# Wider weight rows, shared load slots and a one-row last piece in a decode kernel that streams weights

## Chip, cores, metric

One core of one Trainium2 chip runs the kernel. The metric is device microseconds of one execution. A kernel is executed several times; runs called "fast" are those of the undisturbed state, and all comparisons below use them alone. Kernels timed together share one chip and one set of runs of the kernel before.

## The reference, cut to what matters

```python
# two tokens (batch 2), D = 576, 32 query heads, 16 KV heads, head size 128, last 2048 of 8192 positions
xn  = layernorm(x)
q   = xn @ wq                                  # wq: 576 x 4096
p   = softmax(q . k_cache[:, :, -2048:] * Dh**-0.5)
att = (p . v_cache[:, :, -2048:]) @ wo         # wo: 4096 x 576
h   = relu(xn @ w1 + b1) ** 2                  # w1: 576 x 4608
out = x + att + h @ w2 + b2                    # w2: 4608 x 576
```

Everything is bf16. K, V and the four weight matrices are 53.6 MB and each byte is used once, for two tokens: a kernel that is all loading.

## The kernel before

It works on eight units (four groups of four KV heads, two batches). For each unit it loads K and V (128 partitions, 16 KB rows), transposes K on TensorE, multiplies scores, softmax, and P times V. wq, w1, wo and w2 are loaded between them; w2 comes last. The parts that the change touches:

```python
kvpool = tile_pool(bufs=6)       # K, V and w2 pieces, 16 KB per partition
wbig   = tile_pool(bufs=4)       # full 128-row blocks of wq, later of w1, 9 KB per partition
...
def issue_w(tiles, wt, c, name, width, lrem):
    if c < NFULL:                # NFULL = 4: rows c*128 .. c*128+127, one row to a partition
        tl = wbig.tile([P, WBW], BF16, tag="wbig", name=f"{name}_{c}")
        nc.sync.dma_start(out=tl[:, 0:width], in_=wt[c * P:(c + 1) * P, :])
    ...                          # the last 64 rows of 576 go to a tile of their own
...
W2P = [(0, 0, 9), (0, 9, 18), (1, 0, 9), (1, 9, 15), (1, 15, 18)]   # w2 pieces: half, first and last row of 18
...
for i, w in enumerate(W2P):      # after the last P times V: per row of a piece two 128x2x288 matmuls
    mlp_o(*w, last=(i == len(W2P) - 1))
fin_sb = copy(out_ps); two output DMAs of 1.1 KB
```

All big loads are issued by SyncE on one queue, in program order.

## Time and profile before

| what | before |
|---|---|
| time, median | 137.42 us (137.30 to 137.44, 3 runs) |
| span of the profiled run | 135.6 us |
| DMA engines busy with data (q1) | 94.7% of the span |
| TensorE busy | 76% |
| bytes, mean rate | 53.90 MB, 397 GB/s |
| last data packet (trace) | 131.82 us |
| final copy of the output begins | 132.87 us |

A page shows the span in 40 slices; a digit is the busy share of a slice in tenths.

### The profile page before, as it was taken

What the parts mean: (1) busy time and instruction counts of PE and PEld (TensorE: products, weight loads), DVE (VectorE), ACT (ScalarE), POOL (GpSimd) and SP (SyncE); (2) the same over time, 40 slices, a digit from 0 to 9 for tenths busy, and PEclk for the clock granted to TensorE, in tenths of its full rate; (3) what the DMA queues carried; (4) which work ended last, traced back from release to release, by engine and by line L of the source; (5) the groups of instructions that cost most, each with busy time, mean ns of one, the idle gap of its engine ahead of it and who ended that gap; (6) DMA issues with size and microseconds to landing.
All of it is one profiled execution on the core that took longest, in us unless ns stands there. A gap on an engine that the chain in (4) does not pass through costs nothing.

```text
span 135.6 us, 4461 instructions
## 1 busy us (share of the span) xinstructions
PE 102.5 (76%) x2054; PEld 91.9 (68%) x2054; DVE 53.9 (40%) x124; ACT 43.0 (32%) x47; POOL 10.0 (7%) x31
## 2 busy tenths in 40 slices
PE   1049947599968999879943993999399599768961
PEld 0039947589968999839933993688399479664530
DVE  7502421574352325422653446355634645660001
ACT  6705550165012521004701550272155127110000
POOL 6400000110110001100011001101100110110000
PEclk9999985569855685556985698698559959955599
DMA  5999999999999999999999999999999999999940
GB/s 112 418 419 418 428 442 402 420 429 440 430 393 430 438 411 409 444 425 396 440 440 406 445 420 425 404 443 423 425 430 413 430 415 426 422 410 417 393 166 1
DMA packets 5278, 53.90 MB, mean 397 GB/s; under 512 B 630, under 2 KB 652, under 8 KB 1164
## 3 DMA queue, kind: packets, MB, share of 16 engines
q1 hardware_dynamic: 5188, 53.61, 94.7%
q8 instruction: 16, 0.26, 0.8%
q0 software_dynamic: 64, 0.01, 0.0%
q14 instruction: 2, 0.02, 0.0%
q10 hardware_dynamic: 8, 0.00, 0.0%
HBM read 53.62 MB, written 0.00 MB: 395 GB/s over the span
## 4 chain that ended last, share of the span: by engine, by line
DMA 55%; PE 35%; DVE 3%; issue 2%; POOL 1%; ACT 1%; SPq 1%; POOLq 0%; ACTq 0%
DMA k<-in_A_k_cache_dram 41%; PE kT_ps L237 18%; DMA w<-in_B_w_dram 10%; PE hT_ps L323 5%; DMA b_sb<-in_B_b_dram 4%; PE sc_ps L252 4%; PE out_ps L213 4%; PE oT_ps L289 3%; PE qT_ps L225 1%; ACT kT L240 1%; POOL b_sb L146 1%; DVE l L271 1%; DVE sub L266 1%; SPq L94 0%; DVE fin_sb L414 0%
## 5 line engine op out<-in xcount | busy, mean ns | idle before, releaser
L237 PE MATMUL kT_ps<-ident,k 128*128 128x128 bf16 x512 | 47.3, 260 | 9.9 <-DMA k<-in_A_k_cache_dram 9.9
L237 PEld LDWEIGHTS <-k 128*128 128x128 bf16 x512 | 39.6, 119 | 11.8 <-DMA k<-in_A_k_cache_dram 10.7
L240 ACT COPY kT<-kT_ps 128x1024 bf16<-128x1024 bf16 x32 | 32.3, 1012 | 40.1 <-PE kT_ps L237 40.0
L242 DVE COPY kT<-kT_ps 128x1024 bf16<-128x1024 bf16 x32 | 22.0, 690 | 33.4 <-PE kT_ps L237 33.4
L252 PE MATMUL sc_ps<-qT_all,kT 128*128 128x8 bf16 x512 | 21.6, 168 | 1.6 <-ACT kT L240 0.8
L252 PEld LDWEIGHTS <-kT 128*128 128x128 bf16 x512 | 19.1, 100 | 2.6 <-ACT kT L240 1.2
L289 PE MATMUL oT_ps<-pT,v 128*128 128x8 bf16 x512 | 15.5, 167 | 1.9 <-issue 1.4
L269 ACT ACTIVATE pT<-sub 128x512 bf16<-128x512 f32 x8 | 5.0, 630 | 35.1 <-DVE sub L266 35.1
L289 PEld LDWEIGHTS <-v 128*128 128x128 bf16 x512 | 14.4, 99 | 2.1 <-issue 1.6
L271 DVE TENSOR_REDUCE l<-pT 128x8 f32<-128x512 bf16 x8 | 8.5, 1066 | 4.2 <-ACT pT L269 4.2
L213 PE MATMUL out_ps<-wo,ws 128*2 128x288 bf16 x64 | 8.3, 438 | 2.4 <-DVE ws L309 2.4
L323 PE MATMUL hT_ps<-xnT,w 128*128 128x2 bf16 x144 | 9.8, 201 | 0.0
L323 PEld LDWEIGHTS <-w 128*128 128x128 bf16 x144 | 9.4, 165 | 0.0
L258 DVE TENSOR_REDUCE m<-sc_ps 128x8 f32<-128x512 f32 x8 | 5.5, 692 | 9.7 <-PE sc_ps L252 9.7
L262 POOL PARTITION_ALL_REDUCE gmax<-m x8 | 2.9, 364 | 84.8 <-DVE m L260 84.8
L213 PE MATMUL out_ps<-w,hT_sb 128*2 128x288 bf16 x72 | 6.9, 353 | 1.3 <-DMA w<-in_B_w_dram 1.3
L213 PEld LDWEIGHTS <-ws 128*2 128x2 bf16 x64 | 3.5, 115 | 5.4 <-DVE ws L309 2.8
L213 PEld LDWEIGHTS <-hT_sb 128*2 128x2 bf16 x72 | 3.8, 103 | 4.3 <-issue 1.9
L266 DVE TENSOR_TENSOR sub<-sc_ps,gm 128x512 f32<-128x512 f32 x8 | 5.5, 692 | 0.3
L225 PE MATMUL qT_ps<-xnT,wq 128*128 128x2 bf16 x128 | 4.0, 165 | 2.2 <-DMA wq<-in_A_wq_dram 1.9
L225 PEld LDWEIGHTS <-wq 128*128 128x128 bf16 x128 | 3.9, 103 | 2.2 <-DMA wq<-in_A_wq_dram 2.0
L273 POOL PARTITION_ALL_REDUCE lsum<-l x8 | 3.2, 398 | 24.5 <-DVE l L271 24.5
(58 smaller groups left out, 35.1 us busy)
## 6 DMA issues: line engine op xcount, KB each, us to landing
v<-in_A_v_cache_dram SPq DMA_DIRECT2D x8, 2048.0 KB, 28.4
k<-in_A_k_cache_dram SPq DMA_DIRECT2D x7, 2048.0 KB, 29.4
w<-in_B_w_dram SPq DMA_DIRECT2D x4, 1152.0 KB, 17.7
wo<-in_A_wo_dram SPq DMA_DIRECT2D x4, 1152.0 KB, 27.4
wq<-in_A_wq_dram SPq DMA_DIRECT2D x4, 1024.0 KB, 6.9
w<-in_B_w_dram SPq DMA_DIRECT2D x3, 1296.0 KB, 22.7
k<-in_A_k_cache_dram SPq DMA_DIRECT2D x2, 1024.0 KB, 9.1
w<-in_B_w_dram SPq DMA_DIRECT2D x1, 864.0 KB, 15.7
```

The lines of the kernel that those rows point to most:

```text
L213: nc.tensor.matmul(out_ps[32 * i:32 * i + B, :], lhsT=lhsT, rhs=rhs_of(i * OH, (i + 1) * OH), start=start, stop=stop, skip_group_check=True)
L225: nc.tensor.matmul(qT_ps[:, h, :], lhsT=lhsT, rhs=xnT[:, xc, :], start=(c == 0 and h == 0), stop=(c == KC - 1), skip_group_check=True)
L237: nc.tensor.transpose(out=kT_ps[:, i * P:(i + 1) * P], in_=k_sb[:, j * Dh:(j + 1) * Dh], identity=ident[:])
L240: nc.scalar.copy(out=kT[:], in_=kT_ps[:])
L242: nc.vector.tensor_copy(out=kT[:], in_=kT_ps[:])
L252: nc.tensor.matmul(sc_ps[:, g * JG + i, :], lhsT=kT[:, i * P:(i + 1) * P], rhs=qT_all[:, b, tq * NC:(tq + 1) * NC], start=True, stop=True)
L258: nc.vector.tensor_reduce(out=m1[:], in_=sc_ps[:].rearrange("p j c -> p c j"), axis=AX.X, op=ALU.max)
L266: nc.vector.tensor_tensor(out=sub[:], in0=sc_ps[:], in1=gm2[:].unsqueeze(1).to_broadcast([P, NJ, NC]), op=ALU.subtract)
L269: nc.scalar.activation(out=pT[:], in_=sub[:], func=ACT.Exp, scale=scale)
L271: nc.vector.tensor_reduce(out=l1[:], in_=pT[:].rearrange("p j c -> p c j"), axis=AX.X, op=ALU.add)
L289: nc.tensor.matmul(oT_ps[:], lhsT=v_sb[:, j * Dh:(j + 1) * Dh], rhs=pT_tiles[u][:, j, :], start=(j == 0), stop=(j == NJ - 1))
L323: nc.tensor.matmul(hT_ps[:, s * FR + r, :], lhsT=lhsT, rhs=xnT[:, xc, :], start=(c == 0 and s == 0 and r == 0), stop=(c == KC - 1), skip_g ...
```

## The change

The intent is fewer and larger packets (a packet is the run of bytes, here one row, that a DMA engine moves at a time). The 512 full rows of wq and w1 are laid out as row 4p+i, so that partition p holds rows 4p to 4p+3 and a load can fetch two neighbouring rows as one run of 16 or 18 KB. The activations are transposed with a stride of 4 to match. All big loads share seven 18 KB slots, and the last w2 piece shrinks to one row.

```diff
-    kvpool = ctx.enter_context(tc.tile_pool(name="kvpool", bufs=6))
+    kvpool = ctx.enter_context(tc.tile_pool(name="kvpool", bufs=7))
-    wbig = ctx.enter_context(tc.tile_pool(name="wbig", bufs=NFULL))
+    RP = NFULL // 2
+    SLOT = max(UE, RP * F)
 ...
+    def issue_w(tiles, wt, c0, c1, name, width):
+        if c0 % RP == 0:
+            tiles[c0 // RP] = kvpool.tile([P, SLOT], BF16, tag="kv", name=f"{name}_{c0 // RP}")
+        tl = tiles[c0 // RP]
+        rows = wt[0:NFULL * P, :].rearrange("(p i) l -> p (i l)", i=NFULL)
+        o = (c0 % RP) * width
+        nc.sync.dma_start(out=tl[:, o:o + (c1 - c0) * width], in_=rows[:, c0 * width:c1 * width])
 ...
-        nc.tensor.transpose(out=pro_ps[:, c, :], in_=xn_sb[:, c * P:(c + 1) * P], identity=ident[:B, :B])
+        nc.tensor.transpose(out=pro_ps[:, c, :], in_=xn_sb[:, c:NFULL * P:NFULL], identity=ident[:B, :B])
 ...  (loads: wq row 0, both halves of K 0, wq row 1, wq rows 2-3; w1 rows 0-1, w1 rows 2-3)
-    W2P = [(0, 0, 9), (0, 9, 18), (1, 0, 9), (1, 9, 15), (1, 15, 18)]
+    W2P = [(0, 0, 9), (0, 9, 18), (1, 0, 9), (1, 9, 17), (1, 17, 18)]
 ...  (start: q block 0, all transposes of K 0, then the other q blocks)
```

More of the change, by code (lines that the diff above doesn't have):

```diff
@@ L81 @@
     k_tiles, v_tiles, wq_tiles, w1_tiles, wo_tiles, w2_tiles = {}, {}, {}, {}, {}, {}
-    WBW = max(Hq * Dh, F)
     WRW = max(LQ, L1)
+    RP = NFULL // 2
+    SLOT = max(UE, RP * F)
     def unit_view(cache, u):
@@ L89, in issue_kv @@
     def issue_kv(tiles, cache, u, name, parts=1):
-        tl = kvpool.tile([P, UE], BF16, tag="kv", name=f"{name}_{u}")
+        tl = kvpool.tile([P, SLOT], BF16, tag="kv", name=f"{name}_{u}")
         v = unit_view(cache, u)
@@ L95, in issue_kv, with issue_rem, w_operands @@
                 for i in range(parts)]
-    def issue_w(tiles, wt, c, name, width, lrem):
-        if c < NFULL:
-            tl = wbig.tile([P, WBW], BF16, tag="wbig", name=f"{name}_{c}")
-            nc.sync.dma_start(out=tl[:, 0:width], in_=wt[c * P:(c + 1) * P, :])
-        else:
-            tl = wrem.tile([P, WRW], BF16, tag="wrem", name=f"{name}_rem")
-            nc.sync.dma_start(out=tl[:, 0:lrem], in_=wt[NFULL * P:D, :].rearrange("r (s l) -> (r s) l", s=S))
-        tiles[c] = tl
-    def issue_wq(c):
-        issue_w(wq_tiles, A_wq, c, "wq", Hq * Dh, LQ)
-    def issue_w1(c):
-        issue_w(w1_tiles, B_w1, c, "w1", F, L1)
-    def w_operands(tiles, c, col0, L, step=1):
+    def issue_w(tiles, wt, c0, c1, name, width):
[5 more added lines that the diff above has]
+        nc.sync.dma_start(out=tl[:, o:o + (c1 - c0) * width], in_=rows[:, c0 * width:c1 * width])
+    def issue_rem(tiles, wt, name, lrem):
+        tl = wrem.tile([P, WRW], BF16, tag="wrem", name=f"{name}_rem")
+        nc.sync.dma_start(out=tl[:, 0:lrem], in_=wt[NFULL * P:D, :].rearrange("r (s l) -> (r s) l", s=S))
+        tiles["rem"] = tl
+    def w_operands(tiles, c, col0, width, L, step=1):
         last = col0 + (P - 1) * step
         if c < NFULL:
-            return tiles[c][:, col0:last + 1:step], c
+            o = (c % RP) * width
+            return tiles[c // RP][:, o + col0:o + last + 1:step], c
         sg = col0 // L
         assert last // L == sg
-        return tiles[c][:, col0 - sg * L:last - sg * L + 1:step], NFULL + sg
+        return tiles["rem"][:, col0 - sg * L:last - sg * L + 1:step], NFULL + sg
     def issue_wo(tq):
@@ L126, in issue_w2 @@
     def issue_w2(s, r0, r1):
-        tl = kvpool.tile([P, (r1 - r0) * D], BF16, tag="kv", name=f"w2_{s}_{r0}")
+        tl = kvpool.tile([P, SLOT], BF16, tag="kv", name=f"w2_{s}_{r0}")
         rows = B_w2[s * L1:(s + 1) * L1, :].rearrange("(p r) n -> p (r n)", r=FR)
-        nc.sync.dma_start(out=tl[:], in_=rows[:, r0 * D:r1 * D])
+        nc.sync.dma_start(out=tl[:, 0:(r1 - r0) * D], in_=rows[:, r0 * D:r1 * D])
         w2_tiles[(s, r0)] = tl
@@ L138 @@
     k0 = issue_kv(k_tiles, A_k_cache, 0, "k", parts=2)
-    issue_wq(0)
+    issue_w(wq_tiles, A_wq, 0, 1, "wq", Hq * Dh)
     k0[0]()
-    issue_wq(1)
     k0[1]()
-    for c in range(2, KC):
-        issue_wq(c)
+    issue_w(wq_tiles, A_wq, 1, 2, "wq", Hq * Dh)
+    issue_w(wq_tiles, A_wq, 2, 4, "wq", Hq * Dh)
+    issue_rem(wq_tiles, A_wq, "wq", LQ)
     b1_sb = const.tile([P, S, FR], BF16, name="b1_sb")
@@ L223, in q_block @@
         for h in range(Hq):
-            lhsT, xc = w_operands(wq_tiles, c, h * Dh, LQ)
+            lhsT, xc = w_operands(wq_tiles, c, h * Dh, Hq * Dh, LQ)
             nc.tensor.matmul(qT_ps[:, h, :], lhsT=lhsT, rhs=xnT[:, xc, :],
@@ L321, in mlp_h_block @@
             for r in range(FR):
-                lhsT, xc = w_operands(w1_tiles, c, s * L1 + r, L1, FR)
+                lhsT, xc = w_operands(w1_tiles, c, s * L1 + r, F, L1, FR)
                 nc.tensor.matmul(hT_ps[:, s * FR + r, :], lhsT=lhsT, rhs=xnT[:, xc, :],
@@ L347, in load_v @@
             f()
-    W2P = [(0, 0, 9), (0, 9, 18), (1, 0, 9), (1, 9, 15), (1, 15, 18)]
+    W2P = [(0, 0, 9), (0, 9, 18), (1, 0, 9), (1, 9, 17), (1, 17, 18)]
     load_k(1)
-    issue_w1(0)
-    issue_w1(1)
+    issue_w(w1_tiles, B_w1, 0, 2, "w1", F)
     load_v(0)
     load_k(2)
-    for c in range(2, KC):
-        issue_w1(c)
+    issue_w(w1_tiles, B_w1, 2, 4, "w1", F)
+    issue_rem(w1_tiles, B_w1, "w1", L1)
     load_v(1)
@@ L360 @@
     load_k(3)
-    nxt = {0: [], 1: [], 2: [lambda: load_v(2), lambda: load_k(4)]}
     def step(u, extra=()):
@@ L372, in step @@
         softmax(u)
-    for g in range(4):
+    q_block(0)
+    for g in range(NG):
         transposes(0, g)
-    q_block(0)
-    q_block(1)
-    for g in range(4, NG):
-        transposes(0, g)
-    for c in range(2, KC):
+    for c in range(1, KC):
         q_block(c)
@@ L404 @@
                 load_k(u + 2)
-        if u >= NU - 1:
-            pass
         if u == NU - 1:
```

## The prediction

The medians of 309 to 613 ns are times of packets in the trace of before. For the instruction fetches what stands is the count, 16 packets on q8 for the 4110 TensorE instructions (the page lists 4108); for the clock it is what was granted, 0.50 from 120 to 128 us and 1.00 from 129 us to the last matmul.

> **What bounds the kernel now.** I read the page's slices first, because they say whether one resource is full all the time.
>
> ```profile
> span 135.6 us, 4461 instructions
> PE   1049947599968999879943993999399599768961
> PEclk9999985569855685556985698698559959955599
> DMA  5999999999999999999999999999999999999940
> DMA packets 5278, 53.90 MB, mean 397 GB/s; under 512 B 630, under 2 KB 652, under 8 KB 1164
> q1 hardware_dynamic: 5188, 53.61, 94.7%
> q8 instruction: 16, 0.26, 0.8%
> ```
>
> The DMA row is 9 in every slice from the second to the 38th; the PE row falls to 3 several times. So the sixteen DMA engines set the pace and TensorE waits. 94.7% of 135.6 us is 128.4 us of packets per engine, and the data packets run from about 1.7 us to 131.8 us. There is no hole in the stream that a better order of loads could fill. The second view is the DMA queue's own waits, since the change moves buffers:
>
> ```profile
> SPq L94 <- PE kT_ps L237: 17.0, 3, 6.5
> SPq L129 <- PE kT_ps L237: 14.8, 2, 8.4
> SPq L100 <- PE qT_ps L225: 10.9, 4, 4.5
> ```
>
> These waits look large (10.9 us for w1 loads behind the reads of wq, which the change removes in this form), but a wait of the issuing queue costs time only if the engines run dry, and the slices say that they do not. The page's issue list gives the reserve:
>
> ```profile
> v<-in_A_v_cache_dram SPq DMA_DIRECT2D x8, 2048.0 KB, 28.4
> k<-in_A_k_cache_dram SPq DMA_DIRECT2D x7, 2048.0 KB, 29.4
> w<-in_B_w_dram SPq DMA_DIRECT2D x1, 432.0 KB, 13.0
> ```
>
> A K or V load lands 28 to 29 us after its issue, while 2 MiB (2.097 MB) at some 425 GB/s take 5 us: more than 20 us of other loads stand ahead of it. The third view is the end, as busy time by stretch (PE, PEld, DVE, ACT, POOL with counts, then granted clock, DMA share, GB/s) and as the TensorE timeline:
>
> ```profile
> 110.00:120.00 10.00, 8.38 (x203) 7.89 (x202) 5.19 (x11) 4.68 (x5) 0.38 (x2) 0.84 1.01 425
> 128.00:129.00 1.00, 0.88 (x12) 0.43 (x7) 0.00 (x0) 0.00 (x0) 0.00 (x0) 0.81 0.83 332
> 129.00:130.00 1.00, 0.84 (x14) 0.61 (x15) 0.00 (x0) 0.00 (x0) 0.00 (x0) 1.00 0.58 227
> 130.00:131.00 1.00, 0.43 (x8) 0.17 (x3) 0.00 (x0) 0.00 (x0) 0.00 (x0) 1.00 0.48 183
> 131.00:132.00 1.00, 0.77 (x12) 0.52 (x12) 0.00 (x0) 0.00 (x0) 0.00 (x0) 1.00 0.32 124
> ```
>
> ```profile
> 125.66 3.22 PE L213 MATMUL out_ps<-w,hT_sb 128*2 128x288 bf16 x28
> 129.16 1.27 PE L213 MATMUL out_ps<-w,hT_sb 128*2 128x288 bf16 x18 [0.28 <-DMA w<-in_B_w_dram]
> 131.24 0.90 PE L213 MATMUL out_ps<-w,hT_sb 128*2 128x288 bf16 x12 [0.81 <-DMA w<-in_B_w_dram]
> 132.30 0.53 PE L213 MATMUL out_ps<-w,hT_sb 128*2 128x288 bf16 x6 [0.17 <-DMA w<-in_B_w_dram]
> ```
>
> From 128.5 us the DMA share is about a half: eight engines have finished and eight run 3.1 us longer. Sorting the packet records of the trace into sixteen sequences, each with every load's eight packets in order, I find that the engines ending at 131.7 to 131.8 us each carried two of the 16 instruction fetches (queue q8) and the others none. A fetch leaves a gap of about 1.05 us in the data, and the data packet after it takes up to 0.55 us too long: about 1.55 us each, 3.1 us for two. The kernel's end is the slowest engine's last packet, 0.5 us to landing, six matmuls, and the output.
>
> [...]medians are 309 ns for 8192 B, 349 for 9216, 398 for 10368, 613 for 16384. The line through 9216 and 16384 has 0.0368 ns per byte and some 10 ns left over. [...]PE has 4110 instructions in both kernels, [...]and the trace shows 16 packets of 16384 B on q8. [...]The granted clock of 1.00 at the end and 0.50 from 120 to 128 us [...]matters in the tail below.
>
> **The change, part by part.**
>
> *Wider rows.* w1 used 4 x 128 packets of 9216 B and will use 2 x 128 of 18432 B. From the line an 18432 B packet takes 613 + 2048 x 0.0368 = 688 ns (an estimate; no such packet is in this trace) in place of 2 x 349 = 698. Each engine carries 16 of them: 16 x 10 = 0.16 us. Two wq loads become one with 16384 B rows: 8 packets at 613 in place of 16 at 309, 8 x 5 = 0.04 us. The other two wq loads keep 8192 B. Three loads fewer mean three completion packets of 9 ns fewer per engine: 0.03 us. Bytes are unchanged. Together 0.23 us off every engine, the eight late ones too.
>
> *Row order 4p+i.* The activations are transposed with a stride of 4 to match; counts of matmuls and transposes stay the same, and so do the column strides of the weight loads. Each partition now reads its row from an address 32 or 36 KB after the last one's. K reads at 16 KB steps run at 613 ns, so I take no loss.
>
> *Seven shared slots.* SBUF goes from 6 x 16 + 4 x 9 = 132 KB to 7 x 18 = 126 KB per partition. The second w1 load now waits for the slot of K 0, which is free when its 64 transposes are done, by some 17 us; V 1 and K 3 wait for wq's slots at 18 to 22 us. At that time 15.4 MB have been issued (wq 4.7, K 0 to 2 and V 0 8.4, half of w1 2.4), which last until 1.7 + 15.4/0.425 = 38 us. Later a load waits for the buffer seven loads back in place of six. So the engines stay fed and the value is 0.
>
> *Load and PE order at the start.* TensorE does one q block, all eight transpose groups, then the other q blocks. K 0 arrives whole before the second wq row. TensorE waits for K 1 at 25.9 us in any case, so 0.
>
> *The last w2 piece.* 9+9+9+6+3 rows become 9+9+9+8+1. The packet time is 264 + 139 before and about 349 + 52 after (1152 B, estimated from 31 ns at 576 B and 139 at 3456 B): nothing. But the eight-row piece lands later than the six-row one did. The last landing, 132.26 before, comes at 132.03. The one-row piece takes 8 x 52 + 9 = 0.43 us of its engine, so the eight-row piece lands at 131.60. Its 16 matmuls take 16 x 75 ns (0.90 us for 12 above) = 1.20, and the last two 0.18: end at 132.98, where before it was 132.83. With the last piece so small, its landing no longer sets the end; the eight-row piece does. The cost is 0.38 against the 0.23 won.
>
> Sum: -0.23 + 0.38 = +0.15 us with the full clock. If the half-rate clock (3.22 us for 28 matmuls, 115 ns) covers the tail, 18 x 115 = 2.07 in place of 1.38: another +0.7 us.
>
> **Rivals.** (a) Wide rows run better than the line says, or the freed 10.9 us of queue wait count. Against it: [...]no dry slice. [...](b) The 32 KB step of wq collides in HBM. If wq and w1 (9.4 MB, 22 us) ran 10% slower, the end would move by 2.2 us, to 139.6. Nothing in the trace speaks for it: V, K and wo with different steps all lie on one line. (c) The shared slots starve the queue around 20 to 45 us. A hole would come out one to one in the end, 138 to 140. The 15 MB issued early speak against it. (d) A fetch no longer hits the late engines twice, or the last fetch comes after the data: up to 1.5 us off, to 136. But it needs all eight late engines to change, and the PE instruction count has not. (e) The clock in the tail, above: 138.2.
>
> **Range and chances.** The centre weighs +0.15 us (full clock), +0.85 (half clock, less likely since low activity at the end stood at 1.00 before) and a slightly better packet rate than the line: 137.5 us. The range is 136.9 to 138.2. Two per cent is 2.75 us: [...]for the slower side (b) or (c) would be needed. Faster 0.02, same 0.95, slower 0.03.
>
> **What would show it.** Wide rows: w1 packets of about 688 ns, the DMA row still 9 throughout, GB/s still about 425. Slots: the wait of w1 on the q blocks gone from the queue's waits, replaced by one on the K transposes, with no dip below 0.95 of DMA share before 128 us. Fetches: still 16 on q8, and a half-share tail of about 3 us. Tail: 16 matmuls in one run, the last two following without a wait for w2. A DMA share under 0.9 at 20 to 50 us, packets above 720 ns, or a tail without the late half would prove me wrong.

## More of the kernel before

A framework gives each load one of eight completion counters in turn; a load waits for the load eight places back on its counter, and for the readers of its buffer. (In the trace of before the twelfth load that SyncE issued, K 2, landed at 41.23 us, and the 20th, which waited for it, was issued at 41.25.)

The profile's lines that bound the kernel stand in the prediction. Two more are used later: the chain of work that ended last (start, length, what), and from it how short the part is that no transfer covers.

```profile
119.21 13.05 DMA w<-in_B_w_dram
132.30 0.55 PE out_ps L213 x6
132.87 0.45 DVE fin_sb L414
```

The chain goes through a w2 load for its last 13 us. Then come six matmuls, the copy out of PSUM, the output DMA and the closing of the program.

## The result, and the profile after

The changed kernel took 137.69 us (median of 4, 137.58 to 137.84) and the kernel before 137.43 us on the same chip. The ratio is 1.0018 with a 95% interval of 1.0001 to 1.0036. A ratio is the mean time of one kernel's fast runs over that of the other's of the same rounds, so it is not quite the ratio of the medians. On a second chip the ratio was 0.9995 (0.9976 to 1.0014). So a sign for the whole change is not settled; its parts can be measured.

The page after, in the rows that the prediction showed of before:

```profile
span 136.0 us, 4457 instructions
DMA  4999999999999999999999999999999999999820
DMA packets 4846, 53.90 MB, mean 396 GB/s; under 512 B 582, under 2 KB 732, under 8 KB 988
q1 hardware_dynamic: 4756, 53.61, 93.9%
q8 instruction: 16, 0.26, 0.8%
```

432 packets of q1 are gone (5188 to 4756): 384 of data and 48 completions. The bytes are the same and the DMA row is 9 up to the tail, as before. The instruction queue still has its 16 packets. The queue's own waits (engine, line, what it waited for; us, times, longest) and the issue list changed as foreseen:

```profile
SPq L94 <- DMA k<-in_A_k_cache_dram: 14.8, 4, 4.6
SPq L103 <- PE kT_ps L236: 5.4, 1, 5.4
```

```profile
v<-in_A_v_cache_dram SPq DMA_DIRECT2D x8, 2048.0 KB, 33.1
k<-in_A_k_cache_dram SPq DMA_DIRECT2D x7, 2048.0 KB, 35.3
```

The wait of w1 on the q blocks (10.9 us) has become one of 5.4 us on the transposes of K 0. K and V now land 33 to 35 us after issue in place of 28 to 29: the queue is longer, not the stream faster. The tail, by stretch (columns as in the prediction: busy time of the engines, then granted clock, DMA share, GB/s) and as the TensorE timeline:

```profile
110.00:120.00 10.00, 8.13 (x208) 7.62 (x207) 5.18 (x10) 4.62 (x5) 0.36 (x1) 0.84 1.00 420
128.00:129.00 1.00, 0.43 (x10) 0.19 (x6) 0.00 (x0) 0.00 (x0) 0.00 (x0) 1.00 0.67 274
130.00:131.00 1.00, 0.24 (x4) 0.03 (x1) 0.00 (x0) 0.00 (x0) 0.00 (x0) 1.00 0.47 181
```

```profile
128.97 1.27 PE L212 MATMUL out_ps<-w,hT_sb 128*2 128x288 bf16 x18 [0.57 <-DMA w<-in_B_w_dram]
131.73 1.27 PE L212 MATMUL out_ps<-w,hT_sb 128*2 128x288 bf16 x18 [1.49 <-DMA w<-in_B_w_dram]
```

The half-share tail is still there. The eight-row piece lands at 131.69 and its matmuls begin at 131.73. Its 16 matmuls and the last two run as one group of 18 with no wait between them: the one-row piece has landed before it is wanted. The chain's last three pieces:

```profile
105.68 26.00 DMA w<-in_B_w_dram
131.73 1.28 PE out_ps L212 x18
133.04 0.45 DVE fin_sb L405
```

The copy begins at 133.04, where before it was 132.87. That is +0.17 us. The span grew by 0.36 us, so another 0.19 us lies behind the copy. These are the two profiled executions (137.42 and 137.76 us); the medians differ by 0.26 us. The experiments look for both parts.

### The profile page after: what moved, and what is told of

Read it like the earlier page. It is cut to its first block, busy times and chain, and to the rows that moved or that the text cites. A ratio compares the mean times of both kernels' runs of the same rounds, so it can differ in the third digit from the quotient of the medians.

```text
span 136.0 us, 4457 instructions
## 1 busy us (share of the span) xinstructions
PE 101.4 (75%) x2054; PEld 90.5 (67%) x2054; DVE 54.0 (40%) x124; ACT 42.9 (32%) x47; POOL 10.0 (7%) x31
## 3 DMA queue, kind: packets, MB, share of 16 engines
q1 hardware_dynamic: 4756, 53.61, 93.9%
## 4 chain that ended last, share of the span: by engine, by line
DMA 74%; PE 19%; DVE 2%; ACT 1%; issue 1%; SPq 1%; POOL 0%; POOLq 0%; ACTq 0%
DMA k<-in_A_k_cache_dram 55%; DMA w<-in_B_w_dram 19%; PE kT_ps L236 8%; PE hT_ps L322 5%; PE out_ps L212 2%; PE sc_ps L251 2%; PE oT_ps L288 1%; ACT kT L239 1%; DVE l L270 1%; DVE fin_sb L405 0%; POOL lsum L272 0%; SPq L103 0%; PE wps L305 0%; SPq L122 0%; DVE rr L299 0%
## 5 line engine op out<-in xcount | busy, mean ns | idle before, releaser
L236 PE MATMUL kT_ps<-ident,k 128*128 128x128 bf16 x512 | 45.5, 254 | 8.5 <-DMA k<-in_A_k_cache_dram 8.5
L236 PEld LDWEIGHTS <-k 128*128 128x128 bf16 x512 | 38.4, 117 | 10.3 <-DMA k<-in_A_k_cache_dram 8.9
L251 PEld LDWEIGHTS <-kT 128*128 128x128 bf16 x512 | 18.4, 98 | 5.0 <-ACT kT L239 3.2
L288 PE MATMUL oT_ps<-pT,v 128*128 128x8 bf16 x512 | 15.5, 167 | 1.5 <-DMA v<-in_A_v_cache_dram 0.9
L322 PE MATMUL hT_ps<-xnT,w 128*128 128x2 bf16 x144 | 9.3, 201 | 0.0
```

What stands on the lines that cost most here:

```text
L236: nc.tensor.transpose(out=kT_ps[:, i * P:(i + 1) * P], in_=k_sb[:, j * Dh:(j + 1) * Dh], identity=ident[:])
L251: nc.tensor.matmul(sc_ps[:, g * JG + i, :], lhsT=kT[:, i * P:(i + 1) * P], rhs=qT_all[:, b, tq * NC:(tq + 1) * NC], start=True, stop=True)
L288: nc.tensor.matmul(oT_ps[:], lhsT=v_sb[:, j * Dh:(j + 1) * Dh], rhs=pT_tiles[u][:, j, :], start=(j == 0), stop=(j == NJ - 1))
L322: nc.tensor.matmul(hT_ps[:, s * FR + r, :], lhsT=lhsT, rhs=xnT[:, xc, :], start=(c == 0 and s == 0 and r == 0), stop=(c == KC - 1), skip_g ...
```

## The experiments

Twelve kernels ran, all with correct outputs. "Last packet" is the end of the last data packet in a kernel's trace, "copy" the start of the final copy, "closing" the time from the last output landing to the end of the span. Each row rests on one trace; the changed kernel and e10, which are the same program, differ by 0.29 us in the last packet. Each ratio is to the kernel before on the same chip; e1 to e3 share one chip, e8, e10 and e11 a second, and e12 ran on a third.

| kernel | rows | w2 tail | last packet | copy | copy - packet | closing | ratio to before (95%) |
|---|---|---|---|---|---|---|---|
| before | old | 6+3 | 131.82 | 132.87 | 1.05 | 0.97 | 1 |
| e1 | old | 8+1 | 131.74 | 133.21 | 1.47 | 0.95 | 1.0025 (1.0012-1.0037) |
| e8 | old | 6+2+1 | 131.74 | 132.62 | 0.88 | 0.91 | 0.9973 (0.9953-0.9992) |
| after | new | 8+1 | 131.61 | 133.04 | 1.43 | 1.16 | 1.0018 (1.0001-1.0036) |
| e10, after again | new | 8+1 | 131.32 | 132.73 | 1.41 | 1.14 | 0.9995 (0.9976-1.0014) |
| e2 | new | 6+3 | 131.53 | 132.57 | 1.04 | 1.16 | 0.9992 (0.9979-1.0006) |
| e3 | new | 6+2+1 | 131.51 | 132.35 | 0.84 | 1.08 | 0.9976 (0.9963-0.9988) |
| e11, e3 again | new | 6+2+1 | 131.57 | 132.40 | 0.83 | 1.08 | 0.9958 (0.9941-0.9976) |
| e12, e3 with three small loads | new | 6+2+1 | 131.31 | 132.11 | 0.80 | 0.97 | 0.9946 (0.9932-0.9959) |

Theory A is the prediction's sum: the rows shorten the stream a little and the new split spends it at the end. Theory B was that the slots or the row order cost time and the split nothing.

### e1: the split alone, on the kernel before

```diff
-    W2P = [(0, 0, 9), (0, 9, 18), (1, 0, 9), (1, 9, 15), (1, 15, 18)]
+    W2P = [(0, 0, 9), (0, 9, 18), (1, 0, 9), (1, 9, 17), (1, 17, 18)]
```

> The kernel before with the new w2 split (9+9+9+8+1 rows) and nothing else. Theory A (the split costs at the end what the rows win): the stream ends as before, last data packet 131.8 us, last landing near 132.26; the eight-row piece lands at about 131.8 and is followed by 18 matmuls of 75 ns; matmuls end 0.3 to 0.4 us later than before: 137.7 to 137.8 us, ratio 1.002 to 1.003. Rival B (the shared slots or the row order cost the time, the split nothing): 137.4, ratio 1.000.

137.73 us against 137.36: ratio 1.0025. The TensorE timeline:

```profile
131.90 1.27 PE L213 MATMUL out_ps<-w,hT_sb 128*2 128x288 bf16 x18 [1.52 <-DMA w<-in_B_w_dram]
```

The matmuls of the eight-row piece begin at 131.90, 0.66 us later than those of the six-row one of before (131.24), and there are 18 of them. From last packet to copy it takes 1.47 us in place of 1.05. The split alone costs 0.4 us there, and 0.34 us in the start of the copy (133.21 against 132.87) and in the ratio; B falls.

### e2: rows, slots and order alone

The changed kernel with the old W2P line.

> The changed kernel with the old w2 split (9+9+9+6+3): rows, slots and load order alone. Theory A: last data packet 0.2 us earlier than before (131.6), tail as before: 137.2 us, ratio 0.998 to 0.999. Rival B: 137.6 to 137.7, ratio 1.0015 to 1.002.

137.31 us against 137.36, ratio 0.9992. The interval holds 1, so in the time alone this gain is not shown (0.998 to 0.999 was expected). The timeline shows where it went:

```profile
130.91 0.90 PE L212 MATMUL out_ps<-w,hT_sb 128*2 128x288 bf16 x12 [0.81 <-DMA w<-in_B_w_dram]
132.00 0.53 PE L212 MATMUL out_ps<-w,hT_sb 128*2 128x288 bf16 x6 [0.19 <-DMA w<-in_B_w_dram]
```

The matmuls of each piece begin 0.3 us earlier than before (131.24 and 132.30) and the tail has its old form. The copy begins 0.30 us earlier, but the span ends only 0.10 us earlier. 0.19 us is given back in the closing (1.16 in place of 0.97).

### e3 and e8: a finer tail, with and without the new rows

```diff
+    W2P = [(0, 0, 9), (0, 9, 18), (1, 0, 9), (1, 9, 15), (1, 15, 17), (1, 17, 18)]
```

> The changed kernel with the tail 9+9+9+6+2+1, so that the piece ahead of the last is small too. Theory A: the six-row piece is through before the two-row one has landed, two rows before the last; matmuls end some 0.2 us after the last landing (about 132.05), 0.7 us earlier than in the changed kernel: 136.9 to 137.0, ratio to before 0.996 to 0.997. Rival B (the tail split does not matter): as the changed kernel, 137.7.

> The kernel before with the tail 9+9+9+6+2+1 alone, rows, slots and order as before. Theory A: last landing as before (132.26 to 132.3), the last two matmuls end 0.2 us after it in place of 0.55: 137.0 to 137.1, ratio 0.997 to 0.998. If the finer tail only pays together with the wide rows: 137.4.

e3 took 137.09 us against 137.36 (0.9976), e8 137.20 against 137.49 (0.9973). e3 was expected at 0.996 to 0.997 and missed that by little; e8 was inside its 0.997 to 0.998. The end of e3, the last 18 matmuls in one group and the copy:

```profile
130.90 1.40 PE L212 MATMUL out_ps<-w,hT_sb 128*2 128x288 bf16 x18 [0.81 <-DMA w<-in_B_w_dram]
132.35 0.45 DVE L405 CAST fin_sb<-out_ps 34x288 bf16<-34x288 f32 x1 [9.98 <-PE out_ps L212]
```

In both the copy starts 0.84 to 0.88 us after the last packet. A one-row last piece pays once the piece ahead of it is small too: in e3 the 12 matmuls of the six-row piece have all started (the last at 131.51) when the two-row piece lands at 131.59, and only two matmuls are left for the last landing at 131.98. e8 is e1 with another division of the same rows and is 0.0052 below it in ratio, though on another chip.

### e10, e11: the changed kernel and e3 on the chip of e8

> The changed kernel once more, on the chip of the other three, for their comparison: ratio 1.0015 to 1.0025, as at first.

> The changed kernel with the tail 9+9+9+6+2+1 once more, beside the tail alone: by theory A it is 0.15 to 0.3 us under the tail alone (what the wide rows are worth) and 0.5 to 0.7 us under the changed kernel: ratio to before 0.9955 to 0.997.

The changed kernel gave 137.56 us against 137.49, ratio 0.9995: a miss of the expectation, with a last packet (131.32) 0.29 us earlier than in its first trace. e3 gave 137.12, ratio 0.9958, as expected. That chip's runs of the kernel before spread more (137.38 to 138.10, 11 runs), so the small differences there carry less. e11 is 0.0015 below e8, which is what the rows are worth (0.2 us), but the intervals overlap.

### e9: five slots in place of seven

```diff
-    kvpool = ctx.enter_context(tc.tile_pool(name="kvpool", bufs=7))
+    kvpool = ctx.enter_context(tc.tile_pool(name="kvpool", bufs=5))
```

> The changed kernel with five slots of 18 KB in place of seven. Theory A (slots do not bound: the stream runs 20 to 30 us behind the issue): DMA row still 9 until 128 us, issue to landing of K and V shorter (18 to 28 us), 137.6 to 137.9, ratio 1.001 to 1.003. Rival: the slots are what keeps the engines fed, holes show in the DMA row and the time rises by 2 us or more.

137.72 us, ratio 1.0007 (0.9988 to 1.0027), just under the 1.001 expected; the changed kernel with seven slots gave 0.9995 on this chip (e10), and the intervals overlap. From its page:

```profile
DMA  4999999999999999999999999999999999999820
v<-in_A_v_cache_dram SPq DMA_DIRECT2D x8, 2048.0 KB, 21.1
k<-in_A_k_cache_dram SPq DMA_DIRECT2D x7, 2048.0 KB, 24.8
```

With two slots fewer the time from issue to landing falls from 33-35 to 21-25 us and the DMA row has no hole. The slots set how far ahead loads are issued, and that is not the bound.

### e7: K and V rows of half the length, the change turned round

Every K and V load but the first is cut into two of 8192 B rows.

> The changed kernel with every K and V load but the first cut into two of half the row (8192 B in place of 16384 B): the opposite of the change, at larger scale. By the packet medians each engine has 120 packets of 613 ns replaced by 240 of 309 and 15 completions of 9 ns more: +0.6 + 0.14 = +0.74 us on the stream, last data packet near 132.3, 138.4 us, ratio to before 1.007. If row width matters more than the line says (rival a), +2 us or more[...].

139.14 us, ratio 1.0122 (1.0107 to 1.0137): worse than expected. The last packet is at 132.74, 1.13 us later than in the changed kernel, where the medians gave 0.74. Less 0.14 us for the completions, 120 more packets on each engine cost 0.99 us, 8 ns each. The expected step (2 x 309 - 613 = 5 ns) was low: 309 ns is the most frequent time of the 8192 B packets in the trace of before, but their median there is 311, which gives 9 ns, and in e7 it is 312. By the means (617 ns, and some 315 for the halved rows) the step would be 13 ns, more than the stream shows. The prediction's line, with its 10 ns left over for each packet, is near what was measured: rival (a), that width matters much more than the line says, falls.

### e5: one more instruction fetch

164 useless 2x2 matmuls (80 in TensorE's idle time before 8 us, 12 ahead of each later unit) bring TensorE from 4110 to 4438 instructions; the fetch packets on q8 went from 16 to 17.

```diff
+    idle_pairs(80)
     out_acc(ones_b[:, :], lambda a, z: b2_sb[:, a:z])
 ...
+        idle_pairs(12)
         for g in range(NG + 2):
```

> The changed kernel with 164 useless 2x2 matmuls with their weight loads on TensorE (80 of them in its idle time before 8 us, 12 ahead of each step), 328 instructions more[...]. Theory F (each instruction fetch holds one DMA engine for 1.5 us and the engines with two fetches set the end): 17 packets on the instruction queue, one engine carries three fetches and ends near 133.1, last data packet +1.4 to 1.6 us: about 139.2, ratio to before 1.012 to 1.014. Rival G (eight engines are late for another reason): 16 or 17 fetches, last data packet unchanged, 137.7 to 137.9.

138.82 us, ratio 1.0108 (1.0092 to 1.0123). Page rows and the timeline's last group:

```profile
q8 instruction: 17, 0.28, 0.8%
GB/s 147 412 424 443 414 447 407 429 423 426 435 424 404 435 418 431 407 440 403 443 421 426 431 421 414 425 434 421 440 407 433 408 425 432 411 412 413 297 65 1
132.75 1.27 PE L217 MATMUL out_ps<-w,hT_sb 128*2 128x288 bf16 x18 [1.54 <-DMA w<-in_B_w_dram]
```

The stream moves as fast as before, yet the eight-row piece lands 1.0 us later. In the packet records exactly one engine is busy from 131.6 to 132.6 us; the last packet is at 132.57, +0.96 us. The fetches come at 11.6, 19.9, ... 126.3 us. In the trace of before, and in this one, a fetch packet takes 1.02 to 1.11 us and the data packet that follows it takes 0.46 to 0.55 us too long (0.24 after the last fetch of before, where that packet is small). The fetch times repeat every eight fetches (before: 1061, 1099, 1099, 1086, 1018, 1026, 1074, 1069 ns, then 1060, 1099, 1108, 1086, 1018, 1018, 1074, 1078), as they would if eight engines took them in turn. Rival G falls. The size came out under the 1.4 to 1.6 us expected. The late engines do not end at the same instant, so the one with three fetches need not have been the last of them; that is a likely reason, not shown.

### e4 and e6: eight engines loaded alone, to use the early ones' idle 3 us

e4 put a useless load into 8 partitions ahead of each w2 piece, e6 one into all 128 partitions from a source of 8 x 16 rows; both were meant to be carried by eight engines alone.

```diff
 # e4
+        nc.sync.dma_start(out=tl[0:8, SLOT - n:SLOT], in_=B_w2.rearrange("(p r) n -> p (r n)", p=8)[:, 0:n])
 # e6, ahead of the third piece
+            mixed = B_w2[0:P * FR, :].rearrange("(q e r) n -> e q (r n)", e=8, r=FR)
+            nc.sync.dma_start(out=tl[:, SLOT - 1536:SLOT], in_=mixed[:, :, 0:1536])
```

> The changed kernel with five useless loads ahead of the five w2 pieces, each into only 8 partitions (unused bytes of the same slot): one packet of 8064 to 17280 B for each of eight DMA engines, 1.9 us of packets in all on those eight and none on the other eight. Theory F (eight engines are done 3 us early because they carry no instruction fetch): if the padded eight are the early ones, the last data packet stays at 131.6 and the time at 137.7 (the tail of half share from 128 us gets fuller); if they are the late eight, the last packet and the time move by +1.9 to +2.0 us, to 139.6; a mix of both gives +1.9 with some packets ending at 130. Rival H (all sixteen share one limit, so that any added bytes stretch the stream): +0.95 us, 138.6, whichever eight.

> The changed kernel with one useless load ahead of the third w2 piece, made so that eight engines carry it [...]and its 128 rows of 3072 B go to all 128 partitions: 16 packets of some 119 ns, 1.9 us, on each of those eight, nothing on the others. Theory F: if they are the eight that carry no fetches, last data packet stays at 131.6, time 137.6 to 137.8; if they are the late eight, last packet at 133.5 and 139.6; if mixed, 139.6 as well, with the half-share tail in three steps. Rival H (one shared limit): +0.95 us, 138.6. The pad of the run before wrote eight partitions only and slowed every packet; here no packet of another load should take longer than before (10368 B near 398 ns).

Both missed by far: 144.64 us (ratio 1.0502) and 142.85 us (1.0399). Busy time by stretch of e4, then of e6; the last two columns are DMA share and GB/s:

```profile
110.00:116.00 6.00, 5.67 (x119) 5.53 (x117) 2.90 (x5) 4.05 (x4) 0.00 (x0) 0.88 1.04 425
116.00:122.00 6.00, 3.95 (x137) 3.71 (x137) 3.32 (x9) 0.63 (x1) 0.77 (x2) 0.69 0.97 349
```

```profile
110.00:120.00 10.00, 8.87 (x196) 8.31 (x193) 4.81 (x10) 4.20 (x5) 0.77 (x2) 0.84 1.00 421
120.00:130.00 10.00, 7.20 (x124) 4.76 (x124) 1.96 (x6) 0.48 (x1) 0.40 (x1) 0.66 1.03 295
```

The engines are as busy as before and move much less: 10368 B packets take 467 ns (e4) and 494 ns (e6) in the mean in place of 398, and the 3072 B packets of e6 202 ns in place of the 123 that the line gives (119 was expected). 0.39 MB in e6 cost 5.2 us. The useless 8064 B packets of e4 themselves took 309 ns in the median, which is on the line (307); it was the other loads' packets that got longer. Why they did is not shown, and no run separates the partitions that a useless load writes from the order of its source. The cause of both losses stays open. What the runs were for, which eight engines are the late ones and whether their 3 us can be shared out, stays open.

### e12: turning the completion counters

The closing column of the table needed a cause. At the end SyncE waits for the eight completion counters in a fixed order. From the instruction records of the traces (start relative to the last output landing, in us; 107, 109 and 113 to 118 are the completion counters of these loads, the other numbers are other counters):

```
before: -0.16 wait 116/99   +0.02 wait 117/108  +0.08 wait 118/110  +0.14 wait 111
after:  -0.16 wait 113/109  +0.02 wait 114/107  +0.08 wait 115/100  +0.14 wait 116/99
                            +0.20 wait 117/108  +0.26 wait 118/110  +0.33 wait 111
```

In the changed kernel six of these instructions come after the landing, before it were three, at 0.06 us each. e2 has six, e3 five, e1 three, e8 two: the column closing follows (1.16, 1.08, 0.95, 0.91). Three loads fewer than before had moved the two output DMAs three counters back, from 116 and 117 to 113 and 114. Three useless 64 B loads should turn it on:

```diff
     load_k(3)
+    turn = const.tile([1, 3, 32], BF16, name="turn")
+    for i in range(3):
+        nc.sync.dma_start(out=turn[:, i, :], in_=A_x[0, :, 32 * i:32 * (i + 1)])
```

> The changed kernel with the tail 9+9+9+6+2+1 and three useless loads of 64 B after K 3. Seen in the traces: at the end SyncE waits for the eight completion counters in a fixed order, some 0.06 us each, and in the changed kernel six of these waits come after the output has landed, in the one before three, in the tail alone two, in the changed kernel with the fine tail five. Theory C: loads take the counters in turn, so three more loads bring the output's counter three places on: two waits after the landing, landing to end of span 0.91 us in place of 1.08. The stream pays some 0.02 us. So 0.15 us under the fine tail: 136.9 to 137.0, ratio to before 0.994 to 0.9965. If the closing has another cause, it stays at 1.08 us and the time at 137.1.

136.62 us against 137.39, ratio 0.9946 (0.9932 to 0.9959). Three waits came after the landing, not two, and the closing is 0.97 us in place of 1.08. The two output DMAs did move on by three counters, from 114 and 115 in e3 to 117 and 118, the pair of e8: that part of theory C held. But here the one on 117 landed last, 0.17 us after the one on 118, where in e3 and e8 the higher one was last; so one more wait came after. The rest of its advantage over e3, which put the time below the 136.9 us expected, is a last packet at 131.31, 0.20 us earlier. In its trace the 10368 B packets of w2 took 391 ns in the mean, in e3 398; over the 24 on each engine that is 0.17 us. Why they were shorter is not shown (in e10, with as early a last packet, they took 398). e12 has the lowest ratio, 0.5% below the kernel before, but its interval overlaps that of e11.

## Why the prediction was right, point by point

- The bound. The stream of packets on the DMA engines sets the time. e9 (fewer slots), e7 (more packets, +1.13 us on the stream and +1.2% on the time) and e5 agree.
- Wide rows. The 18432 B packets took 687 ns in the median (693 in the mean; 688 predicted). The last packet moved from 131.76 (mean of before, e1, e8) to 131.51 (mean of after, e2, e3, e10, e11): 0.25 us against 0.23. The traces of one group lie up to 0.29 us apart, so this close a match is partly luck; that the sign is right rests on all five new ones being earlier than all three old ones. The prediction calls 309 ns the median of the 8192 B packets; in its own trace the median is 311. e7 shows that 5 ns for a saved packet was low; here the terms were small enough for it not to matter.
- Row order, slots, order at the start: 0. No run separates the three from the wide rows (e2 has all four); e9 tests the slots alone. Of rival (b), slower loads at the new step, nothing shows: after the change the 8192 B packets, half of them wq's, had a median of 309 ns (311 before), and w1's took the 687 ns above. The w1 wait moved to the K transposes and the second w1 load was issued at 16.2 us (17 predicted), with no hole after it. (The MB issued by then add up to 15.5, not 15.4; nothing hangs on it.)
- The split. +0.38 us predicted; 1.43 us from last packet to copy (mean of after, e1, e10) against 1.05 (before, e2) is +0.38. Its two parts were both off and cancelled: the eight-row piece landed at 131.69 and its first matmul started at 131.73, not 131.60, and 18 matmuls took 1.28 us and not 1.38. That the sum was exact is luck.
- The clock. It was 1.00 in the tail, so the +0.7 us did not come. It can: in e4 the last 18 matmuls took 2.32 us, about as long as the 18 that began at 124.83 us there (2.37), under a granted clock of 0.50. It cannot be said how often it would.
- The fetches. Sixteen, and a half-share tail, as foreseen (16 packets for 4110 TensorE instructions, 17 for 4438 in e5); e5 shows that they set the end of the late engines.
- What was missing is the closing: +0.19 us, with which the sum goes from +0.15 to +0.34 us against 0.36 in the spans. No view of the profile lists it, since waits of SyncE are not busy time; comparing the loads' number modulo eight would have shown it. It is nearly as large as the smaller of the two terms that were worked out. The sum is that of one pair of executions: the medians grew by 0.26 us, and on the second chip the difference was gone (e10), with nearly the same time from packet to copy (1.41 us) and closing (1.14 us), but the last packet 0.29 us earlier. The prediction was right in its mechanism and its class; the closeness of the number is in part chance.

## What to carry to other kernels

Here, with the DMA row full from end to end at 416 to 431 GB/s (stretches of 10 us from 20 to 120 us, both traces), waits of the issuing queue and slot counts were worth nothing (e9); what was left is the time per packet and the few microseconds after the last one. There, lay out the last pieces so that each is computed before the next lands: a small last piece behind a large one only makes the large one the last (the copy began at 133.21 us in e1, and at 132.62 in e8 with the same rows cut finer). Count what comes after the result too, since a changed number of loads can shift the closing waits: here by 0.19 us, nearly what the rows won.
